# Weight chunks loaded and used before later x tiles, and last output rows in column parts

## The chip, the cores and the metric

The kernel runs on one core of one Trainium2 chip. The metric is the device time of one execution in microseconds (us). It is some 1.9 us more than the span of the profile (200.47 against 198.57 in the profiled execution of the kernel before).

Engines are called as in the profile: PE is TensorE, DVE is VectorE, ACT is ScalarE, POOL is GpSimd, SP is the engine that issues most DMAs. "L393" is a line of the kernel; nearly all matmuls carry the line of one helper, so they are told apart by the tiles they read.

## The reference

Two linear attention blocks A and B with their own weights read the same x (2048 by 640, bf16), and a gate per row mixes their results:

```python
g = sigmoid((x * gate_w).sum(-1, keepdims=True))
# for each of A and B: 32 heads of 20 columns
q, k, v = split(x @ wqkv)
phi = lambda t: where(t > 0, t + 1, exp(t)) + 1e-6
kv  = einsum("bhsd,bhse->bhde", phi(k), v);  z = sum over s of phi(k)
o   = (phi(q) @ kv) / (phi(q) . z + 1e-6)
return g * (o_A @ wo_A) + (1 - g) * (o_B @ wo_B)
```

## The kernel before

The kernel records operations with their dependencies, a small list scheduler orders them for each engine, and semaphores are derived. The change touches two ends of it.

The first work is K = x @ wk for the first four row tiles of 128 rows (`kA0` to `kA3`). Each needs its x tile transposed on PE (five 128-column transposes, then a DVE copy to `XT`), and each tile is a sum over five chunks of 128 rows of wk. A tile's two PSUM banks are released by exp on ACT and two DVE operations (`phi_k`). All eight PSUM banks are in use by the end of A's four tiles, so B's tile 0 waits for A's tile 0 to be released. Dummy matmuls (`warm`) go first, to raise PE's clock.

```python
for t in range(4):
    dma("SP",  "xn%d" % t,  XN[:, t, 0:D], xin[128*t : 128*t+128, :], ...)       # x tiles on the SP queue
    dma("ACT", "wkA%d" % t, WK["A"][:, t, :], weights("A", D, t, t+1)[:, 0, :], ...)
dma("ACT", "wkA4", WK["A"][:, 4, :], ...)                                       # wk chunks on the ACT queue
# ... wk of B, DMA transposes of x tiles 4 to 15, all other weights, on the SP queue

warm(6)
transpose_x(0); warm(1); transpose_x(1)
first("A", (0, 0))                              # (row tile, chunk): two matmuls of 320 columns
transpose_x(2)
first("A", (1, 0), (0, 1), (1, 1))
transpose_x(3)
first("A", (2, 0), (2, 1))
first("A", *[(t, c) for c in (2, 3) for t in range(3)])
for t in range(3):
    first("A", (t, 4)); phi_k("A", t, kt["A", t])
first("A", *[(3, c) for c in range(NC)]); phi_k("A", 3, kt["A", 3])
for t in range(4):
    first("B", *[(t, c) for c in range(NC)]); phi_k("B", t, kt["B", t])
```

The last work is the output projection, `final(t)` for 16 row tiles: twenty matmuls of 320 columns into two banks, one eviction of 640 columns on ACT, one store of 160 KB. Four output buffers (`OS`) are used in turn.

## Time and profile before

Three executions took 199.82, 200.29 and 201.01 us. What the reading rests on:

| | before |
|---|---|
| PE busy | 97% of 198.6 us |
| PE's share of the chain that ended last | 93% |
| first matmul on B's wk ("first WKB matmul") | 13.57 us |
| first matmul of the last row tile | 192.67 us |
| end of the span | 198.57 us |

From the page: the busy line of the engines, and the chain of waits that ended last, in shares of the span.

```profile
PE 191.7 (97%) x1373; PEld 133.0 (67%) x1379; DVE 105.5 (53%) x201; ACT 79.5 (40%) x124; POOL 6.0 (3%) x16
...
PE 93%; DMA 3%; ACT 1%; DVE 1%; issue 1%; SPq 0%
```

PE is the limit, and it works nearly without a pause in the middle. The windows view (length, then busy time of PE, PEld, DVE, ACT, POOL, granted clock, DMA share, GB/s) says where it is not busy:

```profile
0.00:14.00 14.00, 10.78 (x71) 6.33 (x72) 3.69 (x9) 3.78 (x5) 2.94 (x14) 1.00 0.92 236
14.00:64.00 50.00, 50.00 (x369) 37.61 (x367) 34.76 (x62) 21.20 (x31) 0.32 (x1) 1.00 0.68 166
...
192.60:198.60 6.00, 2.95 (x22) 1.89 (x20) 0.00 (x0) 1.41 (x2) 0.00 (x0) 1.00 0.16 56
```

So something can be won only in the first 14 us and after the last matmul. The chain in order of time (start, length, what) shows the start:

```profile
1.67 5.76 DMA XN<-in_A_x_dram
7.43 0.05 issue
7.47 0.45 PE ps L471 x5
...
11.50 0.71 ACT EK L497
...
12.24 0.34 DVE EK L501
...
12.60 0.84 DVE FEA L506
13.44 0.14 issue
13.57 86.97 PE ps L393 x662
```

The load of x tile 2 lands at 7.43. Everything that PE does up to 13.21 stands behind its transpose, and then PE waits until 13.57 for the release of A's tile 0. The timeline of ACT and SP (start, length, engine, line, operation) shows the other end:

```profile
195.59 0.70 ACT L808 ACTIVATE OS<-ps 128x640 bf16<-128x640 f32 x1 [2.01 <-PE ps L393]
...
196.32 0.33 SPq L382 DMA_DIRECT2D out_dram<-OS  x1
```

After the last matmul an eviction of 640 columns takes 0.70 us; the store issued at 196.32 is seen by its semaphore at 198.12.

### The profile page before, as it was taken

What the parts mean: (1) busy time and instruction counts of PE and PEld (TensorE: products, weight loads), DVE (VectorE), ACT (ScalarE), POOL (GpSimd) and SP (SyncE); (2) the same over time, 40 slices, a digit from 0 to 9 for tenths busy, and PEclk for the clock granted to TensorE, in tenths of its full rate; (3) what the DMA queues carried; (4) which work ended last, traced back from release to release, by engine and by line L of the source; (5) the groups of instructions that cost most, each with busy time, mean ns of one, the idle gap of its engine ahead of it and who ended that gap; (6) DMA issues with size and microseconds to landing.
All of it is one profiled execution on the core that took longest, in us unless ns stands there. A gap on an engine that the chain in (4) does not pass through costs nothing.

```text
span 198.6 us, 3244 instructions
## 1 busy us (share of the span) xinstructions
PE 191.7 (97%) x1373; PEld 133.0 (67%) x1379; DVE 105.5 (53%) x201; ACT 79.5 (40%) x124; POOL 6.0 (3%) x16
## 2 busy tenths in 40 slices
PE   7699999999999999999999999999999999999993
PEld 2467777777788877888855655455766665566772
DVE  0359888888600000041159999999405369961400
ACT  2055455455311128302255378545233155514221
POOL 5000000000000000500000000000000000000000
PEclk9999999999999999999999999999999999999999
DMA  6999999990011411111135302440110210011021
GB/s 179 307 232 142 282 348 248 293 224 13 3 33 33 36 33 33 36 33 33 38 80 139 144 0 46 122 165 3 45 54 33 69 61 7 0 36 66 33 69 66
DMA packets 26754, 18.96 MB, mean 95 GB/s; under 512 B 15860, under 2 KB 26484, under 8 KB 26740
## 3 DMA queue, kind: packets, MB, share of 16 engines
q1 hardware_dynamic: 26020, 17.94, 35.5%
q10 hardware_dynamic: 720, 0.82, 1.5%
q8 instruction: 11, 0.18, 0.4%
q14 instruction: 3, 0.02, 0.0%
HBM read 10.89 MB, written 4.26 MB: 76 GB/s over the span
## 4 chain that ended last, share of the span: by engine, by line
PE 93%; DMA 3%; ACT 1%; DVE 1%; issue 1%; SPq 0%
PE ps L393 93%; DMA XN<-in_A_x_dram 3%; DVE FEA L506 0%; SPq L382 0%; PE ps L471 0%; ACT EK L497 0%; ACT OS L808 0%; DVE EK L501 0%
## 5 line engine op out<-in xcount | busy, mean ns | idle before, releaser
L497 ACT ACTIVATE EK<-ps 128x640 bf16<-128x640 f32 x32 | 22.3, 703 | 25.9 <-PE ps L393 25.8
L701 ACT ACTIVATE EK<-ps 128x512 bf16<-128x512 f32 x40 | 23.9, 598 | 19.0 <-PE ps L393 19.0
L808 ACT ACTIVATE OS<-ps 128x640 bf16<-128x640 f32 x16 | 11.2, 703 | 33.0 <-PE ps L393 33.0
L393 PE MATMUL ps<-WPA,FEA 128*128 128x320 bf16 x160 | 24.4, 300 | 0.0
L393 PE MATMUL ps<-WPB,FEB 128*128 128x320 bf16 x160 | 24.3, 299 | 0.0
L393 PE MATMUL ps<-XN,FEB 128*128 128x320 bf16 (+1 forms) x160 | 22.8, 301 | 0.0
L393 PE MATMUL ps<-WKA,XT 128*128 128x320 bf16 x160 | 22.7, 300 | 0.0
L393 PE MATMUL ps<-WKB,XT 128*128 128x320 bf16 x160 | 22.4, 299 | 0.2 <-DVE FEA L506 0.2
L393 PE MATMUL ps<-XT,WQA 128*128 128x512 bf16 x95 | 22.0, 380 | 0.5 <-ACT EK L701 0.2
L393 PE MATMUL ps<-XT,WQB 128*128 128x512 bf16 x99 | 22.4, 380 | 0.1
L393 PE MATMUL ps<-XN,FEA 128*128 128x320 bf16 (+1 forms) x160 | 22.3, 300 | 0.0
L393 PEld LDWEIGHTS ps<-XN,FEB 128*128 128x128 bf16 x160 | 18.6, 118 | 3.7 <-DVE ZA L552 0.4
L393 PEld LDWEIGHTS ps<-XN,FEA 128*128 128x128 bf16 x160 | 18.8, 117 | 3.4
L548 ACT ACTIVATE GS<-ps 128x640 bf16<-128x640 f32 x10 | 7.0, 703 | 34.5 <-PE ps L393 34.5
L393 PEld LDWEIGHTS ps<-WPA,FEA 128*128 128x128 bf16 x160 | 15.3, 98 | 7.1 <-issue 0.9
L393 PEld LDWEIGHTS ps<-WKB,XT 128*128 128x128 bf16 x160 | 15.6, 98 | 6.5 <-issue 0.5
L393 PEld LDWEIGHTS ps<-WPB,FEB 128*128 128x128 bf16 x160 | 15.6, 98 | 6.1
L393 PEld LDWEIGHTS ps<-WKA,XT 128*128 128x128 bf16 x160 | 15.5, 98 | 5.9
L393 PEld LDWEIGHTS ps<-XT,WQB 128*128 128x128 bf16 x100 | 11.6, 117 | 9.6 <-issue 0.2
L393 PEld LDWEIGHTS ps<-XT,WQA 128*128 128x128 bf16 x100 | 11.4, 118 | 9.0 <-issue 0.7
L705 DVE TENSOR_SCALAR EK<-EK 128x512 bf16<-128x512 bf16 x40 | 11.3, 291 | 11.0 <-ACT EK L701 9.7
L501 DVE TENSOR_SCALAR EK<-EK 128x640 bf16<-128x640 bf16 x32 | 10.3, 326 | 7.0 <-ACT EK L497 7.0
(53 smaller groups left out, 145.7 us busy)
## 6 DMA issues: line engine op xcount, KB each, us to landing
out_dram<-OS SPq DMA_DIRECT2D x16, 160.0 KB, 1.8
XN<-in_A_x_dram SPq DMA_DIRECT2D x3, 640.0 KB, 5.8
WKA<-in_A_wqkv_dram ACTq DMA_DIRECT2D x5, 160.0 KB, 4.9
WVA<-in_A_wqkv_dram SPq DMA_DIRECT2D x1, 800.0 KB, 9.1
WQA<-in_A_wqkv_dram SPq DMA_DIRECT2D x1, 800.0 KB, 11.1
WVB<-in_B_wqkv_dram SPq DMA_DIRECT2D x1, 800.0 KB, 15.9
WQB<-in_B_wqkv_dram SPq DMA_DIRECT2D x1, 800.0 KB, 13.4
WPA<-wrowsA SPq DMA_DIRECT2D x1, 800.0 KB, 4.3
```

Source lines behind the costliest of these rows:

```text
L393: ins = pe.matmul(o, l, r, start=a, stop=z, tile_position=tp, skip_group_check=True)
L497: "ACT", lambda e: e.activation(ek2(), pair(tile, HALF), ACT.Exp),
L501: "DVE", lambda e: e.tensor_scalar(ek(), ek(), 1.0, EPS, op0=ALU.min, op1=ALU.add), _dve_ns(D, 4),
L548: "ACT", lambda e: e.activation(GS[:, k, :].rearrange("p (h f) -> p h f", f=HALF), pair(tile, HALF), ACT.Copy),
L701: "ACT", lambda e: e.activation(ek(), PS[:, tile.banks[0], :], ACT.Exp), _act_ns(512), reads=[(tile,)],
L705: "DVE", lambda e: e.tensor_scalar(ek(), ek(), 1.0, EPS, op0=ALU.min, op1=ALU.add), _dve_ns(512, 4),
L808: "ACT", lambda e: e.activation(OS[:, os.slot, :].rearrange("p (h f) -> p h f", f=HALF), pair(tile, HALF), ACT.Copy),
```

## The change

The intent: let PE work on tiles 0 and 1 through all five chunks while x tiles 2 and 3 are still under way, and shorten what follows the last matmul by evicting and storing the last rows in column parts. Cut to its core:

```diff
-        NOS = 4
+        NOS = 3
+        OL = sb("OL", [128, D])
@@ first loads
-        for t in range(4):  SP: xn t;  ACT: wkA t
-        ACT: wkA4
+        load_wk("ACT", 0); load_x("SP", 0); load_wk("ACT", 1); load_x("SP", 1)
+        load_wk("ACT", 2); load_wk("SP", 3); load_wk("ACT", 4); load_x("SP", 2); load_x("ACT", 3)
@@ K steps
-        warm(6)
+        warm(7)
         transpose_x(0)
         warm(1)
         transpose_x(1)
-        first("A", (0, 0))
-        transpose_x(2)
-        first("A", (1, 0), (0, 1), (1, 1))
-        transpose_x(3)
-        first("A", (2, 0), (2, 1))
-        first("A", *[(t, c) for c in (2, 3) for t in range(3)])
-        for t in range(3):
+        first("A", (0, 0), (0, 1))
+        warm(1)
+        first("A", (1, 0), (1, 1))
+        first("A", (0, 2), (1, 2), (0, 3), (1, 3))
+        transpose_x(2)
+        for t in (0, 1):
             first("A", (t, 4))
             phi_k("A", t, kt["A", t])
-        first("A", *[(3, c) for c in range(NC)])
-        phi_k("A", 3, kt["A", 3])
+        transpose_x(3)
+        for t in (2, 3):
+            first("A", *[(t, c) for c in range(NC)])
+            phi_k("A", t, kt["A", t])
@@ last row tile: final(15) becomes final_parts(15)
+            for lo, hi, eng, put in ((0, 320, "ACT", 0), (320, 480, "DVE", None), (480, D, "ACT", 320)):
+                ... ten matmuls of hi - lo columns into one bank
+                ... eviction of lo:hi to OL on eng
+                if put is not None: store of columns put:hi
```

More of the change, by code (lines that the diff above doesn't have):

```diff
@@ L412, in bass_gated_mix__linear_attn_block__linear_attn_block__prompt_kernel, with load_x, load_wk @@
         )
-        for t in range(4):
-            dma("SP", "xn%d" % t, XN[:, t, 0:D], xin[128 * t : 128 * t + 128, :], writes=[("XN", t)], us=0.25)
-            dma("ACT", "wkA%d" % t, WK["A"][:, t, :], weights("A", D, t, t + 1)[:, 0, :], writes=[("WK", "A", t)], us=0.25)
-        dma("ACT", "wkA4", WK["A"][:, 4, :], weights("A", D, 4, 5)[:, 0, :], writes=[("WK", "A", 4)], us=0.5)
+        def load_x(eng, t):
+            dma(eng, "xn%d" % t, XN[:, t, 0:D], xin[128 * t : 128 * t + 128, :], writes=[("XN", t)], us=0.25)
+        def load_wk(eng, c):
+            dma(eng, "wkA%d" % c, WK["A"][:, c, :], weights("A", D, c, c + 1)[:, 0, :], writes=[("WK", "A", c)], us=0.25)
+        load_wk("ACT", 0)
+        load_x("SP", 0)
+        load_wk("ACT", 1)
+        load_x("SP", 1)
+        load_wk("ACT", 2)
+        load_wk("SP", 3)
+        load_wk("ACT", 4)
+        load_x("SP", 2)
+        load_x("ACT", 3)
         for c0, c1 in ((0, 1), (1, 3), (3, 5)):
@@ L811, in final, with final_parts, steps @@
             outs.append(dma("SP", "out%d" % t, out[0, 128 * t : 128 * t + 128, :], lambda: OS[:, os.slot, :], reads=[(os,)], us=0.5))
+        def final_parts(t):
+            row = out[0, 128 * t : 128 * t + 128, :]
+            for lo, hi, eng, put in ((0, 320, "ACT", 0), (320, 480, "DVE", None), (480, D, "ACT", 320)):
+                tile = _Tile(1)
+                w = hi - lo
+                def steps(lo=lo, hi=hi, tile=tile, w=w):
+                    return [
+                        (PS[:, tile.banks[0], 0:w], PQ[X][:, k, 128 * t : 128 * t + 128], WP[X][:, k, lo:hi],
+                         X == "A" and k == 0, X == "B" and k == NC - 1, None)
+                        for X in XS for k in range(NC)
+                    ]
+                mms(
+                    "f%d" % t, steps, [("PQS", X, t) for X in XS] + [("WP", X, k) for X in XS for k in range(NC)], [(tile,)],
+                    10 * (w + 6),
+                )
+                name = "oe%d_%d" % (t, lo)
+                if eng == "ACT":
+                    sch.op(
+                        "ACT", lambda e, lo=lo, hi=hi, tile=tile, w=w: e.activation(OL[:, lo:hi], PS[:, tile.banks[0], 0:w], ACT.Copy),
+                        _act_ns(w), reads=[(tile,)], writes=[("OL", lo)], name=name,
+                    )
+                else:
+                    sch.op(
+                        "DVE", lambda e, lo=lo, hi=hi, tile=tile, w=w: e.tensor_copy(OL[:, lo:hi], PS[:, tile.banks[0], 0:w]),
+                        _dve_ns(w), reads=[(tile,)], writes=[("OL", lo)], name=name,
+                    )
+                if put is not None:
+                    outs.append(dma(
+                        "SP", "out%d_%d" % (t, lo), row[:, put:hi], lambda put=put, hi=hi: OL[:, put:hi],
+                        reads=[("OL", c) for c in (0, 320, 480) if put <= c < hi], us=0.3,
+                    ))
         kt = {(X, t): _Tile(2) for X in XS for t in range(4)}
@@ L878, in bass_gated_mix__linear_attn_block__linear_attn_block__prompt_kernel @@
                     final(t)
-        for t in range(4 * NB - 4, 4 * NB):
+        for t in range(4 * NB - 4, 4 * NB - 1):
             final(t)
+        final_parts(4 * NB - 1)
         sch.schedule()
```

## The prediction

> **What bounds the kernel now.** TensorE (PE). The page gives PE 97% busy at full clock; the chain that ended last is 93% PE. By the windows view PE is busy 10.78 of the first 14 us, idles 0.6 us in all from 14 to 192.6, and is busy 2.95 of the last 6. Time can only be won at the two ends.
>
> *Start (timeline, DMA landings).* x tiles 0 to 3 land at 3.9, 4.6, 7.4, 8.3 us on the SP queue; wk chunks 0 to 4 at 3.7, 4.3, 6.5, 7.65, 8.5 on the ACT queue. PE issues a K matmul at 5.4, then sits until x tile 2 lands: the chain shows a 5.76 us DMA of XN ending at 7.43. From 7.47 to 13.21 it has no gap, then waits 0.37 us, until 13.57, for DVE to release the banks of A tile 0 (whose K ended at 11.5; ACT 0.70, DVE 0.33 and 0.83 follow).
>
> *End (timeline).* Last matmul issued 195.26; ACT evicts 640 columns 195.59 to 196.30; output DMA issued 196.32, its semaphore seen at 198.12 (1.80 us).
>
> **The start, changed.** Queue slots and sizes stay, the contents move: chunk 3 takes SP slot 3 (7.43), x2 SP slot 4 (8.31), chunk 4 ACT slot 4 (7.65), x3 ACT slot 5 (8.5). With 136 ns per 320-column matmul and 56 per transpose, from the trace, PE does:
> - tiles 0, 1 by chunks 0, 1 and one dummy: 5.23 to 6.53 (before: two matmuls, then idle)
> - chunk 2: 6.57 to 7.11; chunk 3: 7.47 to 8.02
> - transpose x2: 8.35 to 8.63; chunk 4: to 9.17; transpose x3: to 9.45
> - tiles 2 and 3, 20 matmuls: to 12.17.
>
> Tile 0 is finished at 8.9 instead of 11.5, so its banks are free by 11.5 and the 0.37 us wait goes. First WKB matmul at 12.17 instead of 13.57: **1.40 us** earlier. The seventh dummy fills the 0.45 us gap before x0, at no cost; another fills the wait for x1's eviction. Idle pieces stay under 0.4 us; the Trainium skill ("TensorE: Matmul & The Clock Gate", Part 1) puts the fall to the slow clock at an idle window of about 3.4 us, and the trace agrees: a 2 us gap now keeps full clock. Nothing later waits anew (the first transposed x lands at 13.4; PE needs it at 17.6), so PE carries the 1.40 us to the end.
>
> **The end, changed.** The last tile becomes ten 320-column and twenty 160-column matmuls. 120-column ones run at 52 ns, so I estimate 69 ns: 2.74 us against 2.72. The last eviction has 160 columns: from 703 ns (640) and 598 (512) I estimate 0.31, saving 0.39. The last DMA moves 80 KB: eight packets per engine, 56 ns each now, become half as large; estimate 0.15 saved of 1.80. Together **0.5 us**. Three output slots for four cost nothing (a store lands in 1.8 us, tiles come every 2.7).
>
> **Predicted:** 200.29 - 1.40 - 0.5 = 198.4 us, range 197.7 to 199.2. Faster by over 2%: 0.01; within 2%: 0.98; slower: 0.01.
>
> **Would show it right:** first WKB matmul near 12.2 us; PE gaps of 0.3 to 0.4 us before it, ended by WKA and XN DMAs; ACT's last eviction about 0.31 us; last issue to semaphore about 1.65.
>
> **Would make it wrong:** landings that go by content rather than slot; DVE's new order (x3's eviction ahead of tile 0's release) stalling WKB; 160-column matmuls bound by weight loads; a DMA fixed part that makes its halving worthless (end then gains 0.35).

## The result, and the profile after

The changed kernel took 198.11 us (median of 6 executions, 197.73 to 198.54), the kernel before 200.06 in the same comparison (6 executions, 199.26 to 201.95). The ratio is 0.989 with a 95% interval of 0.984 to 0.994: within 2%, and clear of noise. Here and below a ratio is the mean time of one kernel's fast executions over that of the other's in the same rounds, so it is not quite the ratio of the medians.

The page after, the lines that answer to those above:

```profile
PE 192.9 (98%) x1391; PEld 134.2 (68%) x1391; DVE 105.9 (54%) x202; ACT 79.8 (41%) x125; POOL 6.0 (3%) x16
...
PE 97%; DMA 2%; ACT 0%; issue 0%
```

The chain in order of time:

```profile
0.73 3.29 DMA XN<-in_A_x_dram
4.02 0.05 issue
4.07 0.71 PE ps L483 x5
...
5.74 2.41 PE ps L394 x17
8.15 0.28 PE ps L483 x5
8.43 0.54 PE ps L394 x4
8.98 0.28 PE ps L483 x5
9.26 184.59 PE ps L394 x1342
193.85 0.02 issue
193.87 0.30 ACT OL L846
```

In this execution PE, once x tile 0 is in, never waits for a load again: the chain from 4.07 to 193.85 is PE alone. The first WKB matmul is at 11.81 instead of 13.57. The end, in the timeline of PE, ACT and SP:

```profile
190.93 0.84 PE L394 MATMUL ps<-WPA,FEA 128*128 128x320 bf16 x5
...
193.32 0.51 PE L394 MATMUL ps<-WPB,FEB 128*128 128x160 bf16 x5
...
193.87 0.30 ACT L846 ACTIVATE OL<-ps 128x160 bf16<-128x160 f32 x1 [0.94 <-PE ps L394]
...
194.25 0.33 SPq L383 DMA_DIRECT2D out_dram<-OL  x1
```

The two profiled executions split into three stretches:

| stretch, us | before | after | gain |
|---|---|---|---|
| start to first WKB matmul | 13.57 | 11.81 | 1.76 |
| to the first matmul of the last row tile | 179.10 | 179.12 | -0.02 |
| to the end of the span | 5.90 | 5.36 | 0.54 |

The middle is the same to 20 ns; in all fourteen profiles, whatever the kernel, it lies between 179.10 and 179.12. So the kernels differ only in their start and their end. The start's gain of 1.76 is larger than the 1.40 of the prediction, and the question is whether these two executions stand for the others.

### The profile page after: what moved, and what is told of

The parts are those of the page before. It is cut to its first block, busy times and chain, and to the rows that moved or that the text cites. A ratio compares the mean times of both kernels' runs of the same rounds, so it can differ in the third digit from the quotient of the medians.

```text
span 196.3 us, 3278 instructions
## 1 busy us (share of the span) xinstructions
PE 192.9 (98%) x1391; PEld 134.2 (68%) x1391; DVE 105.9 (54%) x202; ACT 79.8 (41%) x125; POOL 6.0 (3%) x16
## 4 chain that ended last, share of the span: by engine, by line
PE 97%; DMA 2%; ACT 0%; issue 0%
PE ps L394 96%; DMA XN<-in_A_x_dram 2%; PE ps L483 1%; ACT OL L846 0%
## 5 line engine op out<-in xcount | busy, mean ns | idle before, releaser
L394 PE MATMUL ps<-WPA,FEA 128*128 128x320 bf16 (+1 forms) x165 | 24.7, 295 | 0.0
L394 PE MATMUL ps<-WPB,FEB 128*128 128x320 bf16 (+1 forms) x165 | 24.7, 295 | 0.0
L394 PE MATMUL ps<-XT,WQA 128*128 128x512 bf16 x100 | 23.2, 380 | 0.0
L820 ACT ACTIVATE OS<-ps 128x640 bf16<-128x640 f32 x15 | 10.6, 704 | 30.9 <-PE ps L394 30.9
L722 DVE SCALAR_TENSOR_TENSOR FEB<-ps,EK 128x512 bf16<-128x512 f32 x20 | 13.6, 688 | 0.4
```

What stands on the lines that cost most here:

```text
L394: ins = pe.matmul(o, l, r, start=a, stop=z, tile_position=tp, skip_group_check=True)
L722: lambda e: e.scalar_tensor_tensor(out=dst, in0=PS[:, tile.banks[0], :], scalar=0.0, in1=ek(), op0=ALU.max, op1=ALU.add),
L820: "ACT", lambda e: e.activation(OS[:, os.slot, :].rearrange("p (h f) -> p h f", f=HALF), pair(tile, HALF), ACT.Copy),
```

## The experiments

Twelve runs were made, of nine new kernels and the changed one (three runs repeat a kernel), all with correct results. Each call compared its kernels with the kernel before on the same chip; its medians there were 200.15 (first four, chip 8), 199.40 (next four, chip 14) and 199.22 (last four, chip 6), of 11 executions each. So differences between calls of some tenths of a microsecond may come from the chip as well as from chance.

### The start alone

Edit: the kernel before with the new load order, K steps and dummies; the last row tile as before.

> The changed start (load order, K steps, dummies) with the old last tile. My theory: the start is worth 1.4 us (predicted) to 1.75 (first WKB matmul 13.57 -> 11.81 in the two profiles), and it adds to the end's gain. So 1.4 to 1.75 us under before. Rival (part of before's late first WKB matmul in its profile was a slow spell of its first loads, which other executions do not have): only about 0.9 us under before, because with the landings that the changed kernel's profile shows, before's steps would reach WKB at about 12.7 instead of 13.57.

Measured: 198.92 us (median of 6; 198.30 to 199.46) against 200.15; ratio 0.9946, interval 0.9903 to 0.9988. The difference of medians, 1.23, lies between the two theories. In its profile the first WKB matmul is at 11.96, and PE has no gap from x tile 0 on; it comes 0.15 later than in the changed kernel's profile because PE's clock rose later (at 6.29 us by the clock record, against 5.66). So the start alone is faster, but the size is not settled by this run; tail_only, next, says why.

### The end alone

Edit: the changed kernel with the old loads and K steps.

> The old start with the last tile in parts 320, 160, 160 and three output slots. Theory: 0.5 us under before (0.40 from the shorter last eviction, 0.15 to 0.2 from the halved last store, less 0.03 for PE), in the profile from the start of the last tile to the end 5.37 us instead of 5.90. Rival (all gain comes from the start): under 0.1. Its profile is a second sample of the old start: if the slow spell was a chance of one execution, the first WKB matmul comes near 12.7; if it belongs to the old load order, near 13.57 again.

Measured: 198.92 us (median of 6; 198.70 to 200.09), ratio 0.9956, interval 0.9916 to 0.9996. The stretch from the last row tile to the end is 5.36 us, as in the changed kernel and not 5.90: the end's 0.54 is confirmed. The times differ by more, 1.23 by medians, although the rest of this kernel is that of before; so some 0.7 us of that difference is chance in the starts, and the 1.23 of start_only has to be read with the same caution. More telling is the start of this profile, which is a second sample of the old one. Its chain:

```profile
2.13 5.12 DMA XN<-in_A_x_dram
...
7.30 0.45 PE ps L472 x5
...
12.17 0.14 issue
12.30 86.97 PE ps L394 x662
```

The same old steps with the same old loads reach the first WKB matmul at 12.30 here, not at 13.57. Here x tile 2 had landed at 5.90 instead of 7.43, and the chain runs through tile 3, which landed at 7.25. So the same start can differ by 1.27 us with how the loads fall out, and a good part of the 1.76 that the pair of profiles credits to the change is of this kind. The windows view of before's profiled execution showed 237 and 210 GB/s in the stretches 4 to 5 and 5 to 6 us, against 323 and 310 in the changed kernel's: the slow spell is there to see. What causes such spells no run here shows.

### The K steps alone, and the loads alone

Edits: the kernel before with one of the two hunks only.

```diff
# steps_only: the K-steps hunk (with dummies), loads as before
# loads_only: the first-loads hunk, K steps as before
```

> The new K steps and dummies, the loads in the old order. Theory A (steps do it; the load order only permutes what lands in which slot): x2 lands early but is used late, chunk 4 lands last and PE waits for it some 0.4 us; first WKB matmul within 0.2 us of start_only's, so the time within 0.2 us of start_only. Theory B (the load order is what matters, as the change's name says): no more than half of start_only's gain.

> The loads in the new order, the K steps and dummies as before. Theory A: the old steps need x2 before nearly everything, it now lands one slot later, so PE waits longer and the first WKB matmul comes 0.5 to 0.9 us later than with old loads: the time 0.3 to 0.9 us above before. Theory B: at least half of start_only's gain, under before.

Measured, against 200.15:

| kernel | median, us | range | ratio to before, 95% interval | first WKB matmul in its profile |
|---|---|---|---|---|
| steps_only | 199.14 | 198.50 to 200.14 | 0.9967, 0.9925 to 1.001 | 13.24 |
| loads_only | 202.54 (202.03 of the four fast ones) | 200.17 to 204.39 | 1.0086, 1.0028 to 1.0144 (fast executions alone) | 16.94 |
| start_only | 198.92 | 198.30 to 199.46 | 0.9946, 0.9903 to 0.9988 | 11.96 |

The loads in the new order are a loss without the new steps; the steps without the new loads keep most of the gain of medians (1.01 of 1.23), though the interval of that run just includes 1. Theory A has the direction right in both, but its details missed: in the profile of steps_only PE waited 1.31 us for chunk 2 and 0.75 for chunk 3 instead of 0.4 for chunk 4, and the first WKB matmul came 1.28 after start_only's instead of within 0.2. And loads_only lost 1.9 us by the medians of fast executions (2.4 with all six), where theory A expected 0.3 to 0.9. Its PE timeline:

```profile
4.73 0.44 PE L393 MATMUL ps<-WKA,XT 128*128 128x320 bf16 x2
7.95 0.71 PE L482 MATMUL ps<-IDN,XN 128*128 128x128 bf16 x5 [2.78 <-DMA XN<-in_A_x_dram]
...
10.59 6.14 PE L393 MATMUL ps<-WKA,XT 128*128 128x320 bf16 x32
16.93 5.59 PE L393 MATMUL ps<-WKB,XT 128*128 128x320 bf16 x40 [0.20 <-DVE FEA L517]
```

and the windows view of PE (length, busy time, granted clock, DMA share, GB/s):

```profile
6.00:8.00 2.00, 0.05 (x1) 0.77 1.05 365
8.00:10.00 2.00, 2.00 (x11) 0.50 1.44 227
10.00:12.00 2.00, 2.00 (x13) 0.50 0.95 217
12.00:14.00 2.00, 2.00 (x10) 0.52 0.93 178
```

While PE waited for x tile 2 its granted clock fell to half and stayed there until 13.9 us: 320-column matmuls then start every 267 ns instead of every 136. From the landings of this execution the estimate worked out below gives 14.11 for the first WKB matmul at full clock; so by that estimate the low clock cost some 2.8 us. Two of the six executions, with a mean clock of 0.98, were put down as slow; three of the four counted as fast show 0.99, so the ratio mixes the late tile with the clock.

### Is the low clock caused by the wait?

Edit to loads_only: 14 dummy matmuls in the wait.

```diff
         first("A", (0, 0))
+        warm(14)
         transpose_x(2)
```

> loads_only (new loads, old K steps) with 14 dummy matmuls (about 3.0 us) put where PE waits for x2. Theory: loads_only's large loss is two things: x2 lands a slot later (PE idle 3.08 us), and after that idle stretch the granted clock is 0.50 from about 8 to 13.8 us, which costs some 2.8 us. With the stretch filled the clock stays full: first WKB matmul at 14.1 to 14.5 instead of 16.94, no matmul spacing of 267 ns in the trace, time 200.5 to 201.3, and the slow runs of 203 to 204 are gone. Rival (the low clock is a state of the chip, as in other slow runs, not an effect of the idle stretch): the low clock and times up to 204 come in some runs as before.

Measured: 201.62 us (median of 6; 201.06 to 202.16) against 199.40, ratio 1.0113. The clock was 0.999 or 1.000 in all six executions, and the profile shows it full through the stretch that was at half in loads_only:

```profile
8.00:10.00 2.00, 2.00 (x16) 1.00 1.20 296
10.00:12.00 2.00, 2.00 (x20) 1.00 1.04 224
```

So the low clock came with PE standing idle, and the executions near 204 are gone. Two things keep this from being a clean test: the two ran on different chips (8 and 14), and in this profile x tile 2 landed at 6.72 instead of 7.91, so that the wait would have been short without the fill too. The evidence is that the clock fell in the middle of the wait in loads_only, that five of its six executions show a mean clock of 0.992 or less while no execution of before in the same call is under 0.998, and that no execution with the fill is under 0.999. The sizes missed: the time is above the 200.5 to 201.3 expected, and the first WKB matmul came at 15.16, not at 14.1 to 14.5. The dummies began at half rate in this execution and lasted until 9.07, so the fill was longer than the wait. Against before the filled kernel is no better than loads_only (1.0113, and 1.0086 of its fast executions): the fill cost about as much as it saved.

### The added dummies

Edit to the changed kernel:

```diff
-        warm(7)
+        warm(6)
...
         first("A", (0, 0), (0, 1))
-        warm(1)
```

> The changed kernel without its two added dummy matmuls (six at first instead of seven, none between tile 0's and tile 1's first matmuls). Theory: they fill waits of 0.2 to 0.45 us, far shorter than the stretch that lowered the clock, so they are worth nothing: first WKB matmul at 11.7 to 12.2, time within 0.3 us of the changed kernel (198.1), clock full in all runs. Rival (they are needed to lift or keep the clock): first WKB matmul 0.4 us or more later, time at least 0.4 us up.

> The changed kernel without the two added dummies again. In its first profile the matmuls stayed at half rate until 9.9 us (267 ns spacing of 320 columns) and the execution took 200.29, the other six 197.8 to 198.4. Theory: with six dummies PE is idle 0.9 us before x0 and the clock's rise then sometimes comes some 4 us late; so again none, one or two of six executions near 200, the others level with the changed kernel. Rival (the two dummies are needed in every execution): the median is up by 0.4 us or more.

Measured: 198.03 us (median of 7; six of them 197.82 to 198.40, the profiled one 200.29), and 198.22 (median of 6; 197.39 to 198.32). The 13 executions have a median of 198.08, the changed kernel's 12 have 198.18: the two dummies show no gain in the median. The first theory's "clock full in all runs" failed, though, in the profile of the 200.29 execution:

```profile
4.17 0.71 PE L483 MATMUL ps<-IDN,XN 128*128 128x128 bf16 x5 [0.69 <-DMA XN<-in_A_x_dram]
...
5.64 4.47 PE L394 MATMUL ps<-WKA,XT 128*128 128x320 bf16 x16
9.91 0.50 PE L483 MATMUL ps<-IDN,XN 128*128 128x128 bf16 x5
...
13.79 0.43 PE L394 MATMUL ps<-WKB,XT 128*128 128x320 bf16 x2
```

Sixteen matmuls fill the 4.27 us from 5.64 to 9.91, which is 267 ns each: the clock was at half until 9.9 us. In the profile of the second call the rate was at half until 6.35 us, so that only the first four of the sixteen matmuls are slow:

```profile
5.49 2.76 PE L394 MATMUL ps<-WKA,XT 128*128 128x320 bf16 x16
```

No execution of the changed kernel took as long as 200.29, but only two of its 12 were profiled. One late clock in 13 executions without the two dummies does not prove that they prevent it.

The edit taken to its end is to drop all the dummies, `warm(7)`, `warm(1)` and `warm(1)`.

> The changed kernel with no dummy matmul at all, so PE's first work is x0's transpose at about 4 us. Theory: the clock rises by recent activity, so now in every execution it stays at half until 8 to 11 us; the work until the first WKB matmul (about 6.4 us at full rate) then ends at 12.4 to 13.9 instead of 11.8; time 198.8 to 200.3, median 0.7 us or more over the changed kernel. Rival (the outlier without dummies was a chance event unrelated to them): within 0.3 us of the changed kernel.

Measured: 199.06 us (median of 6; 198.43 to 199.66), against 198.28 for the changed kernel. Its profile:

```profile
3.76 1.52 PE L483 MATMUL ps<-IDN,XN 128*128 128x128 bf16 x10 [3.76 <-DMA XN<-in_A_x_dram]
5.08 4.47 PE L394 MATMUL ps<-WKA,XT 128*128 128x320 bf16 x16
9.34 0.52 PE L483 MATMUL ps<-IDN,XN 128*128 128x128 bf16 x5
...
13.24 0.98 PE L394 MATMUL ps<-WKB,XT 128*128 128x320 bf16 x6
```

The clock was at half until 9.3 us, as expected, and this in an execution whose loads landed early. The set of dummies is worth about 0.8 us by medians (0.55 by means, six executions each, so the size is rough); the seventh and the ninth are not shown to add to it.

### The last store in one piece, and other parts

Edits to the changed kernel:

```diff
# one_store: the parts as they are, one store of all 640 columns at the end
-            ... ((0, 320, "ACT", 0), (320, 480, "DVE", None), (480, D, "ACT", 320)):
+            ... ((0, 320, "ACT", None), (320, 480, "DVE", None), (480, D, "ACT", 0)):
# parts_480_160: two parts, each stored alone
+            ... ((0, 480, "ACT", 0), (480, D, "ACT", 480)):
# (cut: the list of parts that a store reads follows)
```

> The changed kernel with the parts 320, 160, 160 evicted as now but stored in one piece of 640 columns at the end. It measures what the halved last store is worth. Theory: issue of the last store to its semaphore 1.80 us as in the kernel before, instead of 1.59, so start of the last tile to end is 5.37 + 0.2 = 5.57 us. Rival (a fixed part rules, the size does not matter): 5.37 to 5.42.

> The changed kernel with the last rows in two parts, 480 (ACT) and 160 (ACT), each stored alone, so the last store has 40 KB in rows of 320 bytes. PE: 2.03 + 0.69 us as good as unchanged; eviction 0.30 as now. If the store goes on falling with its size (16 columns' packets at 32 ns are now 8 per engine), last issue to semaphore 1.45 to 1.5 and start of the last tile to end 5.25[...].

The times (199.17 and 198.28) say little, for the start varies; the stretches from the first matmul of the last row tile do not:

| us from the first matmul of the last row tile | before | one_store | after | 480 + 160 |
|---|---|---|---|---|
| last matmul issued | 2.58 | 2.67 | 2.67 | 2.65 |
| last store issued | 3.65 | 3.27 | 3.32 | 3.25 |
| last store's semaphore seen | 5.45 | 5.06 | 4.91 | 4.82 |
| end of the span | 5.90 | 5.51 | 5.36 | 5.27 |
| store alone, issue to semaphore | 1.80 | 1.79 | 1.59 | 1.57 |

The lines from the view of the output tensor, last store of before, then of one_store:

```profile
DMA to landing us min/median/max: 1.8/1.8/1.8
```

```profile
DMA to landing us min/median/max: 1.8/1.8/1.8
```

and of the changed kernel:

```profile
DMA to landing us min/median/max: 1.6/1.6/1.6
```

Halving the last store is worth 0.20 us in the store. At the end 0.15 remain, because SP issues the store 0.05 later: in the changed kernel a second wait, a semaphore instruction of its own, comes before the issue. In the 480 + 160 version SP has one wait only, and the end is 0.09 to 0.10 earlier again; the store itself gains just 0.02 to 0.03 from another halving, where about 0.1 was expected. The trace shows why that halving is no clean test: this store is issued 0.43 us after that of the first 480 columns, and its packets begin (195.16 in after_480_160) as that store's end (195.18), 0.90 us after its issue, against 0.83 in the changed kernel. Its own packets then take 0.28 us, against 0.38 for 80 KB and 0.60 for 160 KB.

### The changed kernel and the best version, once more

> The changed kernel once more, unedited, for more executions beside the next three. All executions between 197.5 and 198.6, none slow, because its seven dummies lift the clock by about 5.6 us in each. In the profile the middle (first WKB matmul to start of last tile) is 179.1 us and the last tile to the end 5.36 us, as in the profiles so far.

> The candidate to beat both: the changed kernel with the last rows in two parts of 480 and 160 columns, each evicted by ACT and stored alone; its one look had 5.27 us from the start of the last tile to the end instead of 5.36. Expected 0.1 us under the changed kernel (198.0), which its spread of some 0.3 us may hide; the 5.27 us again in the profile.

Measured: the changed kernel 198.28 us (median of 6; 197.67 to 199.42), the 480 + 160 version 198.22 (median of 6; 197.47 to 199.04), ratios to before 0.9958 (0.9921 to 0.9995) and 0.9944 (0.9908 to 0.9979). The end of the second is 5.26 us in its profile, against 5.37. That version is faster by 0.1 us where it can be seen, in the profile; the times cannot tell the two apart. My expectation that no execution of the changed kernel would pass 198.6 was wrong: 199.11 and 199.42 came. The second is the profiled one, and in it x tile 3 landed at 9.86 instead of 8.36 and the first WKB matmul came at 12.91. Its PE timeline has the waits for loads that the first profile lacked:

```profile
7.53 1.26 PE L394 MATMUL ps<-WKA,XT 128*128 128x320 bf16 x8 [0.43 <-DMA WKA<-in_A_wqkv_dram]
...
9.90 0.45 PE L483 MATMUL ps<-IDN,XN 128*128 128x128 bf16 x5 [0.18 <-DMA XN<-in_A_x_dram]
```

The reason given was wrong too: seven dummies do not lift the clock by about 5.6 us in each execution. By the clock records it rose at 5.66 (after), 5.96 (after_again), 6.29 (start_only), but at 4.18 in one_store and 3.41 in steps_only, all with the same seven dummies from 0.77 us on.

### The start, worked out from the landings

How late the start is follows from when loads land. From the trace: 0.045 us from a landing to PE, 0.28 us for a tile's transposes, 0.136 us for each 320-column matmul, 0.37 us of wait at the end of the old steps. Counting what must follow each load gives an estimate of the first WKB matmul, at full clock:

- old start: x2 + 6.14, or x3 + 5.04 (0.045 + 0.28 + 32 x 0.136 + 0.37), whichever is later (the chunks can add to it in the same way)
- new start: taken as never under 11.81 (PE's own work, as in the changed kernel's profile; this moves with the clock's rise, and start_only, also without a gap, has 11.96); x2 + 3.86, x3 + 3.04 (0.045 + 0.28 + 20 x 0.136), chunk 3 + 4.41 and so on

With the landings of each slot of the two queues (us; "slot 3" is the third load on that queue), five traces:

| trace | SP 3 | SP 4 | ACT 3 | ACT 4 | ACT 5 | old, est. | new, est. | seen |
|---|---|---|---|---|---|---|---|---|
| before | 7.43 | 8.31 | 6.53 | 7.65 | 8.52 | 13.57 | 12.17 | 13.57 (old) |
| tail_only | 5.90 | 7.25 | 6.77 | 8.43 | 9.32 | 12.29 | 12.36 | 12.30 (old) |
| after | 6.57 | 7.69 | 5.75 | 7.25 | 8.36 | 12.73 | 11.81 | 11.81 (new) |
| one_store | 7.88 | 8.79 | 6.52 | 8.06 | 8.96 | 14.02 | 12.66 | 12.67 (new) |
| after_again | 6.61 | 7.81 | 7.49 | 8.96 | 9.86 | 12.85 | 12.90 | 12.91 (new) |

The estimate meets what was seen to 0.02 us in these. The rows before and after are no test, since the 0.37 and the 11.81 come from them. Of the other traces, start_only is missed by 0.15, and those with a low or late clock (loads_only, loads_filled, no_dummies, all_dummies_off) by more. Over the landings of all fourteen traces, if each slot's landing does not depend on what it carries, its mean is 12.85 for the old start and 12.16 for the new: a gain of 0.70, from -0.1 to 1.4 by the execution. With the new steps and the old loads the mean is 12.44; with the new loads and the old steps 14.12, before the clock falls. So by this estimate the steps give 0.4 and the loads another 0.3 once the steps are there.

## Why the prediction was right

It named 198.4 us with a range of 197.7 to 199.2. The two medians are 198.11 and 198.28. Point by point:

- *PE is the limit, and gains at the two ends arrive in full.* Right: the middle is 179.10 to 179.12 us in every profile.
- *The end gains 0.5 us.* Right: 5.90 to 5.36. Its terms: eviction 0.31 estimated, 0.30 measured; store 1.65 estimated, 1.59 measured; PE 0.02 more estimated, and the last matmul is issued 0.09 later but is itself shorter. 160-column matmuls start every 69 ns, as estimated, half of the 136 of 320-column ones, so weight loads did not bind them.
- *Three output slots cost nothing.* Nothing in the middle moved, so right.
- *"Queue slots and sizes stay, the contents move."* As far as the runs can tell: the third slot of SP landed from 5.9 to 7.4 with x tile 2 in it and from 5.4 to 7.9 with chunk 3. But the slots' times, which the prediction read off one trace, vary by more than a microsecond between executions.
- *"First WKB matmul at 12.17 instead of 13.57: 1.40 us earlier."* The mechanism held, and the size of the gain was off. The pair of profiles shows 1.76. Over executions it is less: in the two calls that ran both kernels the medians differ by 1.95 and 0.94. Pooled, 39 of the kernel before have a median of 199.40 and a mean of 199.72, 12 of the changed kernel 198.18 and 198.28, so the whole gain is 1.2 by medians and 1.4 by means. Less the end's 0.54, the start is worth 0.7 to 0.9; the estimate from the landings gives 0.70. The term that was mis-sized is the old start, not the new one: six profiles with the new loads, steps and dummies reach WKB at 11.81 to 12.91, 12.21 in the mean, close to the 12.17 predicted, while the old start's 13.57 was a late one (12.30 in tail_only, 12.85 in the estimate's mean). The gain taken off was therefore too large, but it was taken from 200.29, the median of three executions that were above the later ones (199.40). That the two errors nearly cancel, and the level came out right, is in part luck.
- *"PE gaps of 0.3 to 0.4 us before it, ended by WKA and XN DMAs."* None in the profile of the result, where loads landed early. In after_again, the same kernel, PE is idle 0.43 us for a chunk and 0.18 for x tile 3, in one_store 0.65 for a chunk and 0.19 for x tile 2. They belong to some executions.
- *"Idle pieces stay under 0.4 us", so the clock stays full.* No execution of the changed kernel was seen with a fallen clock (0.999 is the lowest mean), though an idle piece reached 0.6 us (counted, here and below, from the last matmul's start plus its 136 ns; the timeline, which models a matmul's end, has some 0.16 less). loads_only shows the danger that was passed over in one line: with the wait at 2.94 us the clock fell to half. In before it stayed full over 1.97 us, from 5.51 to 7.48; between the two nothing was measured.

The danger named as "DVE's new order stalling WKB" did not come: in the changed kernel's profiles no wait stands before the first WKB matmul.

## What to carry to other kernels

Order the first work so that whatever lands last has the least work behind it: x tile 2 had 6.1 us of PE work behind it before and has 3.9 now, and that, rather than the load order by itself, is the gain at the start. Take more than one profile before putting a number on a stretch that waits for loads, and use the stretches that do not vary (here the middle and the end, to 20 ns) to separate small effects that whole times hide. When a reordering lengthens a wait of PE, count what a halved clock would cost after it: in loads_only that was some 2.8 us by estimate, about as much as the whole wait of 2.94.

## What the Trainium skill lacked or had wrong

- "TensorE: Matmul & The Clock Gate", Part 1 and the closing table ("Why this matters for your kernels"): an idle window of about 3.4 us, and advice against idle gaps over about 3 us. In loads_only PE was idle from 5.01 to 7.95 us, 2.94 in all, and by the clock record the clock fell to half at 7.08, after about 2.1 us of idling; matmuls 267 ns apart after it confirm the half rate. In the profile of before 1.97 us of idling did not lower it. A limit of 3 us is not safe here.
- The same page, Part 1, on the rise: about 4 us into sustained activity, give or take 0.5 us from run to run. With dummies from 0.77 us on the clock records here put it between 3.41 us (steps_only) and 6.35 us (no_dummies_again), so 2.6 to 5.6 us after the first matmul, a wider spread than the page gives; start_only, whose timeline shows no PE gap from the first dummy on, rose at 6.29. With six dummies and an idle stretch before x tile 0 one execution stayed at half until 9.9 us. That a gap within the warm-up causes such a delay is not shown by one execution, and no page speaks of it.
- No page says, beyond a general caution about clock events on the same page, that the granted clock in the views can read 1.00 while PE still runs at half rate at the start of an execution: in no_dummies it reads 1.00 from 4 to 10 us with 267 ns between 320-column matmuls. The record of that trace, like three others, has no clock entry within the span at all, and the rest have none before the first rise (4.91 us in before). The spacing of matmuls has to be used there.
- "ScalarE: Activation LUTs", What ACT_TABLE_LOAD costs: 186 + 0.833 N ns for an activation with immediate operands gives 319 for 160 columns and 719 for 640. Measured 304 and 703, so the slope agrees and the constant is 15 smaller.
- "DMA: Bandwidth & Descriptors", Anatomy of one DMA: about 2.0 us fixed plus bytes over 436 GB/s, fitted to another issue path. Here SP's last stores took 1.80 us for 160 KB, 1.59 for 80 and 1.57 for 40. The first step agrees with the slope (80 KB over 436 GB/s is 0.19); with that slope the fixed part is nearer 1.4. By the packets of before's last store it is 1.2: 0.83 us from the issue to the first packet and 0.37 from the last packet to the semaphore. The 40 KB store waited behind another, so these runs do not show what is to be won below 80 KB.
- The same page's Specifications ask for 512 bytes or more for line rate. A store of 320-byte rows took 1.57 us against 1.59 with 640-byte rows, but it has half the bytes. Its packets took 20 ns each, against 32 for 640 bytes and 55 for 1280, so per byte they were a quarter slower than those of 640 bytes; no sharp fall shows at this size of 40 KB.
- No page tells how much first loads vary between executions of one kernel: the third load of the SP queue landed from 5.4 to 7.9 us over fourteen profiles.
